# Pooled attention, routed experts and a dense layer in one kernel: scatters at spaced steps of their own, row squares on ScalarE, key differences and PV's evacuation one step up

## The chip, the cores and the metric

One core of a Trainium2 chip runs the whole program in one launch. The metric is the device time in microseconds (us) of one execution; lower is better. Engines are named as in the profile: PE (TensorE matmul), PEld (its weight loads), DVE (VectorE), ACT (ScalarE), POOL (GpSimd), SP (SyncE, which issues most DMAs).

## What is computed

The reference chains three blocks. Attention has 4 batches of 8 heads, 1152 rows of 64, and queries pooled by two (so 576 output rows a head). A router then sends each of the 2304 rows of 512 to one of 8 experts; last comes a dense layer with a squared ReLU.

```python
q_pool = q.reshape(B, H, S // 2, 2, D).mean(axis=3)
scores = scale * np.matmul(q_pool, k.transpose(0, 1, 3, 2))
attn = softmax(scores); x = attn @ v          # rows to (B*S/2, 512)
xn = x / (norm(x) + 1e-6); logits = xn @ en.T / tau
e = argmax(logits); y = gate[e] * (relu(x @ w1[e]) @ w2[e])
h = y @ w_in; out = (relu(h) ** 2) @ w_out
```

## The kernel before, in words

The order of the work is written out by hand. `Attention.run` lays every piece of work at a pair (step, rank), sorts the pairs and emits them. A pair of heads `h` (16 of them, called a head below) owns 18 steps that begin at step 18·h; parts of it lie earlier or later by the offsets of the table `PLAN`. Each engine takes its own instructions in the order in which they were emitted, and waits for the others by semaphores.

In one step of a head the PE makes a tile of scores (`scores`, two PSUM banks `st` in turn), ACT takes the exponential (`exps`, L412), and DVE or POOL makes the low half of the result (`low`, L422, `pl`). PV (L459) follows from step 13 in three groups of six steps; `evac` (L481 to L500) then divides a group by its row sums on DVE and writes it to `xb` (the rows of the batch): four instructions spread over two steps, of which `rs`, `rc` come first and the write `xb` a step later. Meanwhile the next head is prepared: `prep` splits keys, queries and values in a high and a low half (ACT L237, DVE L239), and `smax` finds each row's maximum: PE L338 multiplies queries with the keys and with `kd`, the difference of two halves of the keys (`kdiff`, DVE L315); ACT L361 (`rd`) and DVE L364 fold them to maxima.

When a batch is done (after heads 3, 7 and 11) a generator, `Route.steps`, takes its rows through the router, one piece at each step of the list `PLAN["route"]`, at rank 7, behind the step's other work: the row square sums `sq` (DVE, L661), `scale` (L898, L901), a high half on ACT (`hi`, L674) and a low half on DVE (`lo`) in the tile `xhl`, a transpose, the logits, `choose` (ten small pieces, the last writes the row indices `ri`) and then `scatter` (L761): an indirect DMA issued by POOL for each of 4 or 5 tiles, one a piece. `xhl` has a single buffer for all batches, so that `hi` of a batch waits for the scatters of the one before. In steps of the program these pieces lie so:

| batch | squares | scatters before | scatters in the change | `hi` of the next batch |
|---|---|---|---|---|
| 0 | 90 to 93 | 134, 135, 135, 135 | 135, 138, 141, 144 | 168 |
| 1 | 159 to 163 | 224 to 228 | 225, 227, 229, 231, 233 | 239 |
| 2 | 231 to 234 | 264, 265, 265, 266 | 266, 268, 270, 272 | behind the attention |

Behind batch 2's pieces follows `Moe.begin`: seven pieces that find the fullest expert, at steps 266 to 269 before. The SP reads its number and loads that expert's weights (`wraw`), which ACT splits (`wkr`, L1610) between the exponentials of the last head. The last batch goes through the router behind the attention (with squares of 384 columns). From about 500 us on come the experts and the dense layer, which no edit touches.

Of the kernel before, what the change touches and what calls it, by code (L numbers as in the profile page):

```python
# [10 lines left out]
BF16 = mybir.dt.bfloat16  # L11
I32 = mybir.dt.int32
U32 = mybir.dt.uint32
ACTF = mybir.ActivationFunctionType
ALU = mybir.AluOpType
# [88 lines left out]
        ],  # L104
    ],
    "due": [6, 10, 6],
    "init": [
        44, 45, 46, 47, 48, 49, 50, 51, 52, 53, 54, 55, 56, 57, 58, 59, 60, 61, 62, 63,
# [27 lines left out]
class Attention:  # L136
# [3 lines left out]
    def __init__(self, ctx, kctx, pctx, tc, q, k, v, xbp, xdone):  # L140
        self.tc, self.nc = tc, tc.nc
        self.q, self.k, self.v = q, k, v
        self.xdone = xdone
        B, H, S, D = q.shape
        assert S == 1152 and D == 64
        self.B, self.H = B, H
        self.HP = H // 2
        self.NP = B * self.HP
        pool = lambda n, b, **kw: ctx.enter_context(tc.tile_pool(name=n, bufs=b, **kw))
        keys = lambda n, b: kctx.enter_context(tc.tile_pool(name=n, bufs=b, side="right"))  # L150
        self.raw = keys("raw", 1)
        self.row = keys("row", 1)
        self.t1p = keys("t1", 3)
        self.r2p = pool("r2", 2)
        self.pp = pool("pp", 22)
        self.sm = pool("sm", 2)
        self.xbp = xbp
        self.per = pool("per", 1)
        psum = lambda n, b: pctx.enter_context(tc.tile_pool(name=n, bufs=b, space=PSUM))
        self.ps_t = psum("ps_t", 2)  # L160
        self.ps_m = psum("ps_m", 4)
        self.ps_v = psum("ps_v", 2)
        self.t2 = [self.per.tile([128, 18, 128], F16, name=f"t2_{i}") for i in range(2)]
        self.qr2 = [self.per.tile([128, 9, 128], F16, name=f"qr2_{i}") for i in range(2)]
        self.vx = [self.per.tile([128, 18, 130], F16, name=f"vx_{i}") for i in range(2)]
        self.st = {}

    def init(self):
        V = self.nc.gpsimd
# [137 lines left out]
    SMAX = [(n, m) for r in ((0, 1, 2, 3), (4, 5, 6, 7), (8,)) for n, m in  # L307
            [(r, 2)] + [(n, m) for n in r for m in (1, 0)]]

    def kdiff(self, h):  # L310

        s = self.st[h]
        kd = s["kd"] = self.sm.tile([128, 2, 512], BF16, tag="m24", name="kd")
        t1 = s["t1"].rearrange("p (a c) b -> p a (c b)", a=2)
        self.nc.vector.tensor_tensor(  # L315
            out=kd, in0=t1[:, :, 512:1024], in1=t1[:, :, 0:512], op=ALU.subtract
        )

    def smax(self, h, i):
# [195 lines left out]
    def steps(self, h):  # L515

        t = dict(PLAN["mid"], **PLAN.get(h, {}))
        t["pv"] = [[13 + 6 * g + m for m in range(6)] for g in range(3)]
        t["evac"] = [[13 + 6 * g + 6, 13 + 6 * g + 8] for g in range(3)]
        if h == self.NP - 2:  # L520
            t["evac"][2] = [31, 31]
        if h == self.NP - 1:
            t["pv"] = [[13 + m for m in range(9)]] * 3
            t["evac"] = None
        return 18 * h, t

    def run(self, extra):

        ev = {}

        def at(u, rank, f):
            ev.setdefault(u, []).append((rank, len(ev[u]) if u in ev else 0, f))

        def spread(u, rank, f):

            box = []

            def step():
                if not box:
                    box.append(f())  # L540
                next(box[0], None)

            for k in range(7):
                at(u + k // 3, (rank, 4.6, 6.5)[k % 3], step)

        for u, f in extra:
            at(u, 8, f)
        for h in range(self.NP):
            e0, t = self.steps(h)
            at(e0 + t["load"], 0, lambda h=h: self.load(h))  # L550
            at(e0 + t["load_v"], 0, lambda h=h: self.load_v(h))
            for n, d in enumerate(t["prep"]):
                at(e0 + d, 5, lambda h=h, n=n: self.prep(h, n))
            at(e0 + t["t2"], 0, lambda h=h: self.copy_t2(h))
            for i in range(21):
                u = e0 + (i if i < 18 else t["x"][i - 18])
                at(u - 1, 1, lambda h=h, i=i: self.scores(h, i))
                at(u, 2, lambda h=h, i=i: self.exps(h, i))
                at(u + 1, 6, lambda h=h, i=i, dve=i in t["low"]: self.low(h, i, dve))
            at(e0 + t["smax"][0], 4.4, lambda h=h: self.kdiff(h))  # L560
            for i, u in enumerate(t["smax"]):
                at(e0 + u, 4.5, lambda h=h, i=i: self.smax(h, i))
                spread(e0 + u + 1, 2.2, lambda h=h, i=i: self.smax_red(h, i))
            for g in range(3):
                k = len(t["pv"][g])
                for m, u in enumerate(t["pv"][g]):
                    a, b = (27 * m) // k, (27 * (m + 1)) // k
                    at(e0 + u, 4, lambda h=h, g=g, a=a, b=b: self.pv(h, g, a, b))
                if t["evac"]:
                    f = lambda h=h, g=g: self.evac(h, g)  # L570
                    if h == self.NP - 2 and g == 2:
                        at(e0 + t["evac"][g][1], 2.6, lambda f=f: list(f()))
                    else:
                        spread(e0 + t["evac"][g][1], 2.6, f)
            if h % self.HP == self.HP - 1 and h < self.NP - 1:
                box = []

                def step(b=h // self.HP, box=box):
                    if not box:
                        box.append(self.xdone(b))  # L580
                    next(box[0], None)

                for k in PLAN["route"][h // self.HP]:
                    at(e0 + 33 + k, 7, step)
        for u in sorted(ev):
            for _, _, f in sorted(ev[u], key=lambda t: t[:2]):
                f()
# [17 lines left out]
ORDER = ((0, 1, 2, 3), (0, 1, 2, 3, 4), (0, 1, 2, 3), (0, 4, 1, 2, 3))  # L605
# [39 lines left out]
class Route:  # L645
# [12 lines left out]
    def sq(self, i, cols=slice(0, 512), add=0.0):  # L658
        n = cols.stop - cols.start
        x = self.tiles[i][:, cols]  # L660
        self.nc.vector.tensor_tensor_reduce(  # L661
            out=self.t([512], "sq", BF16)[:, 0:n], in0=x, in1=x, scale=1.0, scalar=add,
            op0=ALU.mult, op1=ALU.add, accum_out=self.m.ss[:, self.s0 + i:self.s0 + i + 1],
        )

    def scale(self, a=0, b=None):
# [104 lines left out]
    def steps(self):  # L771

        n = self.n
# [23 lines left out]
                step += 4  # L797
                due[i] = step + PLAN["due"][BASE.index(self.s0)]
        yield from self.choose()
        for i in range(n):  # L800
            self.scatter(i)
            yield


class Moe:
# [906 lines left out]
def build(tc, q, k, v, emb, tau, w1, w2, w_in, w_out, consts, at, out):  # L1712
    nc = tc.nc
    pool = lambda c, n, b, **kw: c.enter_context(tc.tile_pool(name=n, bufs=b, **kw))
    with ExitStack() as ctx, tc.manual_schedule():
# [3 lines left out]
        with ExitStack() as actx:  # L1719
# [10 lines left out]
            def xdone(b):  # L1730
                xts = lambda i: rb.tile([128, 8, 128], F16, tag="xT", name="xT", bufs=2)
                xhl = rb.tile([128, 5, 1024], F16, tag="xhl", name="xhl")
                yield from route(b, slice(0, len(ORDER[b])), xts, xhl).steps()
                if b == 2:
                    yield from moe.begin(small)

# [146 lines left out]
```

## Time and profile before

| | us |
|---|---|
| median of three timed runs | 1180.41 |
| lowest and highest of them | 1174.77, 1183.54 |
| the profiled execution, its own time | 1168.99 |
| its span in the profile | 1167.0 |
| attention, first to last exponential | 25.1 to 464.7 |

The span is that of the profiled execution; 1.99 us lie outside it. In rows of a timeline the numbers are start and duration in us, and a bracket says how long the engine had been idle and who released it. In a row that groups instructions the numbers behind the bar are busy us and the mean duration in ns. Rows of a head's window run from its first exponential to that of the next head, 18 steps.

### The profile page before, as it was taken

To read this page: it belongs to the slowest core of one execution; us is meant where nothing else is said; L and a number is where in the kernel's file an instruction comes from. 1 tells how busy PE (TensorE), PEld (TensorE's weight loads), DVE (VectorE), ACT (ScalarE), POOL (GpSimd) and SP (SyncE) were. 2 spreads that over 40 slices of the span, in tenths; PEclk is the share of its full clock that TensorE was granted. 3 is DMA by queue.
4 is the path that set the end of the run, shared out by engine and by line. 5 is a ranking of instruction groups with operands and counts; after the bars stand their busy time and mean duration, and the time that the engine had idled before them with its cause. 6 is when DMAs were issued, how large, how long until landed. Compare 5 with 4: busy or idle time off the path is not lost. (4 is left out here: it accounts for less than half of the span.)

```text
span 1167.0 us, 28582 instructions
## 1 busy us (share of the span) xinstructions
PE 1046.6 (90%) x11297; PEld 702.0 (60%) x11340; DVE 734.8 (63%) x1403; ACT 521.7 (45%) x972; POOL 519.3 (45%) x454
## 2 busy tenths in 40 slices
PE   6889999988999798999998869787879999999996
PEld 2455665655666466999898858654435454555543
DVE  6898999999999988866654547958822121211200
ACT  4777777767777566323222325533303131221300
POOL 3655564555666456522442336826623232232300
PEclk7899998999999898999999889989889999999999
DMA  7555875755675435659558595323300000000000
GB/s 195 141 130 145 201 169 108 170 147 118 140 151 150 72 96 161 166 176 224 103 111 210 135 256 167 89 72 111 111 19 10 19 10 10 19 10 19 1 28 27
DMA packets 166245, 128.17 MB, mean 110 GB/s; under 512 B 125208, under 2 KB 129432, under 8 KB 166064
## 3 DMA queue, kind: packets, MB, share of 16 engines
q1 hardware_dynamic: 160304, 107.91, 39.0%
q0 software_dynamic: 5760, 17.85, 5.0%
q8 instruction: 113, 1.85, 0.7%
q14 instruction: 68, 0.56, 0.2%
HBM read 74.69 MB, written 12.60 MB: 75 GB/s over the span
## 5 line engine op out<-in xcount | busy, mean ns | idle before, releaser
L422 POOL TENSOR_TENSOR pl<-p 128x512 f16<-128x512 f32 x144 | 167.9, 1170 | 176.2 <-ACT p L412 173.3
L394 PE MATMUL st<-r,t 128*128 128x64 f16 (+3 forms) x1152 | 202.6, 299 | 5.4 <-ACT p L412 4.7
L412 ACT ACTIVATE p<-st 128x512 f32<-128x512 f32 x288 | 168.5, 595 | 78.9 <-PE st L394 77.1
L1465 PE MATMUL a<-yT,win 128*128 128x384 f16 x1056 | 178.5, 332 | 16.8 <-ACT r L1470 11.8
L459 PEld LDWEIGHTS <-p 128*128 128x128 bf16 x2304 | 135.6, 99 | 68.1 <-issue 18.5
L1465 PEld LDWEIGHTS <-win 128*128 128x128 f16 (+1 forms) x1152 | 114.8, 100 | 97.3 <-issue 27.1
L459 PE MATMUL pv<-vx,p 128*128 128x65 f16 x2250 | 160.0, 197 | 9.5 <-DVE xb L500 9.5
L1543 PE MATMUL o<-wo,gh 128*128 128x512 f16 (+1 forms) x513 | 154.5, 380 | 5.7 <-ACT wo L1168 4.2
L459 PE MATMUL pv<-vx,pl 128*128 128x65 f16 x1125 | 144.9, 194 | 0.0
L422 DVE TENSOR_TENSOR pl<-p 128x512 f16<-128x512 f32 x144 | 141.8, 985 | 1.0 <-ACT p L412 0.7
L1470 ACT ACTIVATE r<-a 128x384 f32<-128x384 f32 x88 | 42.9, 487 | 194.8 <-PE a L1465 128.7
L1483 POOL TENSOR_TENSOR gl<-r,gh 128x384 f16<-128x384 f32 x88 | 87.3, 997 | 79.8 <-ACT gh L1482 79.8
L1471 DVE TENSOR_TENSOR r<-r 128x384 f32<-128x384 f32 x88 | 59.5, 676 | 100.2 <-ACT r L1470 100.2
L364 DVE CUSTOM_DVE_ANT_0 rd<-sm,rd,mc 128x512 bf16<-128x512 f32 x144 | 106.7, 744 | 22.4 <-PE sm L338 9.1
L1405 PE MATMUL fsm<-x,ws 128*128 128x192 f16 (+1 forms) x1344 | 104.7, 241 | 17.6 <-issue 9.8
L1550 DVE TENSOR_SCALAR ot<-o,cms 128x512 f32<-128x512 f32 x18 | 13.5, 751 | 166.5 <-PE o L1543 166.5
L394 PEld LDWEIGHTS <-t 128*128 128x128 f16 (+1 forms) x1152 | 77.0, 100 | 66.5 <-issue 32.0
L1405 PEld LDWEIGHTS <-ws 128*128 128x128 f16 (+1 forms) x1344 | 100.6, 101 | 20.8 <-issue 12.2
L459 PEld LDWEIGHTS <-pl 128*128 128x128 f16 x1152 | 111.0, 101 | 0.0
L361 ACT ACTIVATE rd<-sm 128x512 bf16<-128x512 f32 x144 | 85.5, 597 | 52.7 <-PE sm L338 43.6
L1417 PEld LDWEIGHTS <-ws 128*128 128x128 f16 (+1 forms) x1344 | 97.5, 99 | 18.1 <-issue 14.5
L1417 PE MATMUL fst<-hl,ws 128*128 128x192 f16 (+1 forms) x448 | 96.9, 236 | 12.7 <-issue 8.8
(249 smaller groups left out, 1735.3 us busy)
## 6 DMA issues: line engine op xcount, KB each, us to landing
stg<-in_moe_w SPq DMA_DIRECT2D x24, 1024.0 KB, 7.7
vr<-in_v SPq DMA_DIRECT2D x16, 576.0 KB, 4.2
kr<-in_k SPq DMA_DIRECT2D x15, 576.0 KB, 5.3
fill<-in_moe_w_in POOLq DMA_DIRECT2D x16, 512.0 KB, 7.0
g<-in_moe_w_out SPq DMA_DIRECT2D x16, 512.0 KB, 3.5
qr<-in_q SPq DMA_DIRECT2D x15, 512.0 KB, 5.7
t<-t SPq DMA_DIRECT2D x16, 288.0 KB, 3.8
xs<-tmp SPq DMA_DIRECT2D x16, 192.0 KB, 2.8
```

The source lines that it names most:

```text
L361: nc.scalar.activation(out=s["rd"], in_=ps, func=ACTF.Relu)
L364: nc.vector.tensor_tensor_reduce(out=rd, in0=ps, in1=rd, scale=1.0, scalar=mc[:, slots:slots + 1], op0=ALU.add, op1=ALU.max, accum_out=mx[ ...
L394: nc.tensor.matmul(out=st[:, j * n:j * n + n], lhsT=lhs[0:kk, m, :], rhs=r[0:kk, c0:c0 + n], start=first, stop=(kk == 65), skip_group_chec ...
L412: nc.scalar.activation(out=p, in_=st[:, 0:p.shape[1]], func=ACTF.Exp, scale=SCALE)
L422: eng.tensor_tensor(out=pl, in0=s.pop(("p32", i)), in1=s["ph", i], op=ALU.subtract)
L459: nc.tensor.matmul(out=o[:, 0:vn], lhsT=s[p, i][:, cs:cs + w], rhs=vx[:, 9 * a_ + c, v0:v0 + vn], start=(u == 0 and p == "ph" and v0 == 0) ...
L1405: self.nc.tensor.matmul(out=ps[:, f, 0:w], lhsT=w1(wh, f2)[:, fs], rhs=x[:, 4 * xh + k, 0:w], start=(f == 0 and m == 0), stop=(m == 11), s ...
L1417: self.nc.tensor.matmul(out=yp[m // 2][:, m % 2, 0:w], lhsT=w2(wh, f)[:, ds], rhs=h(l, f), start=(f == i == m % 2 == 0), stop=(f == 7 and ...
L1465: nc.tensor.matmul(out=ps, lhsT=half(self.win[wh][:, k, fs], wh), rhs=self.yT[yh][:, k, c0], start=(m == 0), stop=(m == 11),)
L1471: nc.vector.tensor_tensor(out=r, in0=r, in1=r, op=ALU.mult)
L1483: self.nc.gpsimd.tensor_tensor(out=lo, in0=g, in1=hi, op=ALU.subtract)
L1543: nc.tensor.matmul(out=ps, lhsT=at(l, f)[:, rs], rhs=half(wout[wh][:, f], wh), start=(m == 0), stop=(m == 47),)
```

## The change

There are four edits. `scatter` leaves the generator: `run` emits it at steps of its own (`PLAN["scatter"]`, rank 7.5, with the object kept in `att.routes`); `Moe.begin`, which came behind the scatters, moves up by two steps (264 to 267). The 13 squares of 512 columns of batches 0 to 2 become one ACT instruction each with its accumulator; each took two on DVE, the product and the reading of the accumulator. `kdiff` is emitted one step earlier, and for head 0 in two halves. All of `evac` moves up by one step (its first instruction from eight to seven steps behind the group's first PV step), save that of head 14's last group.

```diff
+    "scatter": [[48, 51, 54, 57], [66, 68, 70, 72, 74], [35, 37, 39, 41]],
...
-    def kdiff(self, h):
+    def kdiff(self, h, a=slice(0, 2)):
...
-        kd = s["kd"] = self.sm.tile([128, 2, 512], BF16, tag="m24", name="kd")
+        if a.start == 0:
+            s["kd"] = self.sm.tile([128, 2, 512], BF16, tag="m24", name="kd")
...
-            out=kd, in0=t1[:, :, 512:1024], in1=t1[:, :, 0:512], op=ALU.subtract
+            out=s["kd"][:, a], in0=t1[:, a, 512:1024], in1=t1[:, a, 0:512], op=ALU.subtract
...
-        t["evac"] = [[13 + 6 * g + 6, 13 + 6 * g + 8] for g in range(3)]
+        t["evac"] = [13 + 6 * g + 7 for g in range(3)]
...
-            at(e0 + t["smax"][0], 4.4, lambda h=h: self.kdiff(h))
+            if h:
+                at(e0 + t["smax"][0] - 1, 4.4, lambda h=h: self.kdiff(h))
+            else:
+                for i, a in ((0, slice(0, 1)), (9, slice(1, 2))):
+                    at(e0 + t["smax"][i], 4.4, lambda a=a: self.kdiff(0, a))
...
+                for i, k in enumerate(PLAN["scatter"][h // self.HP]):
+                    at(e0 + 33 + k, 7.5, lambda b=h // self.HP, i=i: self.routes[b].scatter(i))
...
+        if n == 512:
+            self.nc.scalar.activation(out=out, in_=x, func=ACTF.Square, accum_out=ss)
+            return
...
-        for i in range(n):
-            self.scatter(i)
-            yield
```

PE and SP keep their instructions and their order. On POOL, around the scatters of batch 0 (`pl`, `plx` are low halves, `qs` the query sums of the next head), the order before was:

```order
L422 TENSOR_TENSOR pl<-p_4657 128x512
L761 DMA xs<-xhl,ri 18432x1024 x4
L422 TENSOR_TENSOR pl<-p_4724 128x512
L422 TENSOR_TENSOR pl<-p_4804 128x512
L422 TENSOR_TENSOR plx<-p32x 128x384
L259 TENSOR_TENSOR qs<-qr 128x576
L422 TENSOR_TENSOR pl<-p_4858 128x512
```

and it is now, at the same place:

```order
L425 TENSOR_TENSOR pl<-p_4660 128x512
L774 DMA xs<-xhl,ri 18432x1024
L425 TENSOR_TENSOR pl<-p_4726 128x512
L425 TENSOR_TENSOR pl<-p_4796 128x512
L425 TENSOR_TENSOR plx<-p32x 128x384
L774 DMA xs<-xhl,ri 18432x1024
L261 TENSOR_TENSOR qs<-qr 128x576
L425 TENSOR_TENSOR pl<-p_4853 128x512
L774 DMA xs<-xhl,ri 18432x1024
L425 TENSOR_TENSOR pl<-p_4934 128x512
```

Three of the four scatters went behind low halves that used to follow them. On DVE, where batch 1's squares began (`mc`, `rs`, `rc` small; `xb<-pv,rc` the write of PV's last group of the batch), the order before was:

```order
L373 TENSOR_SCALAR qr_0_105<-mx 128x4
L355 TENSOR_REDUCE mc<-sm 128x4
L481 TENSOR_SCALAR rs<-pv 128x3
L485 RECIPROCAL rc<-rs 128x3
L239 SCALAR_TENSOR_TENSOR krow<-kr,krow 128x9x64
L422 TENSOR_TENSOR pl<-p_5482 128x512
L661 ISA sq,ss<-xb 128x512
L661 ISA ss 128x1
L500 TENSOR_TENSOR xb<-pv,rc 128x3x64
L661 ISA sq,ss<-xb 128x512
L661 ISA ss 128x1
L364 ISA rd,mx<-sm,rd,mc 128x512
```

and it is now:

```order
L484 TENSOR_SCALAR rs<-pv 128x3
L488 RECIPROCAL rc<-rs 128x3
L376 TENSOR_SCALAR qr_0_105<-mx 128x4
L358 TENSOR_REDUCE mc<-sm 128x4
L503 TENSOR_TENSOR xb<-pv,rc 128x3x64
L241 SCALAR_TENSOR_TENSOR krow<-kr,krow 128x9x64
L425 TENSOR_TENSOR pl<-p_5483 128x512
L367 ISA rd,mx<-sm,rd,mc 128x512
```

The write to `xb` went ahead of a key split and a low half, and the squares are gone. They stand on ACT now, each ahead of an exponential:

```order
L364 ACTIVATE rd<-sm 128x512
L239 ACTIVATE krow<-kr 128x9x64
L673 ACTIVATE sq,ss<-xb 128x512
L415 ACTIVATE p_5586<-st 128x512
L673 ACTIVATE sq,ss<-xb 128x512
L415 ACTIVATE p_5612<-st 128x512
L364 ACTIVATE rd<-sm 128x512
```

The second square of a batch (in batches 1 and 2 the first too) waits for DVE's write to `xb`; the exponentials stand behind it.

## Rows read from the trace of the kernel before

**Rows 1.** The page's busy time by engine.
```profile
PE 1046.6 (90%) x11297; PEld 702.0 (60%) x11340; DVE 734.8 (63%) x1403; ACT 521.7 (45%) x972; POOL 519.3 (45%) x454
```

**Rows 2.** Windows by head: us, busy PE PEld DVE ACT POOL, clock, DMA, GB/s.
```profile
138.10:162.60 24.50, 23.93 (x378) 15.76 (x377) 22.71 (x51) 19.45 (x38) 15.71 (x13) 1.00 0.73 167
162.60:192.10 29.50, 26.55 (x377) 16.79 (x375) 27.10 (x59) 20.69 (x40) 14.90 (x13) 0.88 0.52 121
...
243.40:272.90 29.50, 25.53 (x377) 16.36 (x375) 27.39 (x59) 19.52 (x38) 16.74 (x15) 0.94 0.47 112
272.90:303.00 30.10, 25.64 (x374) 16.20 (x373) 28.87 (x65) 20.61 (x39) 16.46 (x13) 0.94 0.55 119
...
354.10:379.90 25.80, 23.92 (x384) 15.77 (x383) 24.47 (x57) 18.75 (x35) 15.69 (x15) 1.00 0.66 173
379.90:414.50 34.60, 26.83 (x383) 16.97 (x383) 32.66 (x68) 20.42 (x39) 16.93 (x16) 0.85 0.44 81
```

**Rows 3.** Waits of the PE, 0 to 430 us: total us, times, longest.
```profile
PE sm L338 <- DVE kd L315: 15.1, 13, 3.0
PE pv L459 <- DVE xb L500: 9.5, 7, 5.1
PE sm L338 <- DVE mx L364: 7.7, 6, 3.3
```

**Rows 4.** Timeline of the PE: five of those waits.
```profile
13.34 0.58 PE L338 MATMUL sm<-kd,r 128*128 128x512 bf16 x1 [3.01 <-DVE kd L315]
...
177.80 0.61 PE L338 MATMUL sm<-kd,r 128*128 128x512 bf16 x1 [2.27 <-DVE kd L315]
...
246.92 0.38 PE L338 MATMUL sm<-kd,r 128*128 128x512 bf16 x1 [3.27 <-DVE mx L364]
...
289.47 0.61 PE L338 MATMUL sm<-kd,r 128*128 128x512 bf16 x1 [1.99 <-DVE kd L315]
...
387.43 0.27 PE L459 MATMUL pv<-vx,p 128*128 128x65 f16 x2 [5.14 <-DVE xb L500]
```

**Rows 5.** Timeline of DVE: one low half as usual, four stretched instructions.
```profile
236.98 0.69 DVE L422 TENSOR_TENSOR pl<-p 128x512 f16<-128x512 f32 x1
...
238.60 7.59 DVE L422 TENSOR_TENSOR pl<-p 128x512 f16<-128x512 f32 x1
...
378.88 3.73 DVE L373 TENSOR_SCALAR qr<-mx 128x4 f16<-128x4 f32 x1
...
383.38 2.51 DVE L239 SCALAR_TENSOR_TENSOR krow<-kr,krow 128x576 f16<-128x576 f32 x1
...
441.67 4.97 DVE L422 TENSOR_TENSOR pl<-p 128x512 f16<-128x512 f32 x1 [0.15 <-ACT p L412]
```

**Rows 6.** Timeline of POOL around batch 0's scatters: first scatter, the train behind.
```profile
232.62 1.12 POOL L761 DMA_INDIRECT xs<-xhl,ri  x1 [2.02 <-DVE ri L756]
...
237.69 2.05 POOL L422 TENSOR_TENSOR pl<-p 128x512 f16<-128x512 f32 x2
...
244.61 1.03 POOL L422 TENSOR_TENSOR pl<-p 128x512 f16<-128x512 f32 x1
```

**Rows 7.** The squares on DVE (ns: shortest, median, longest); ACT instructions of their size.
```profile
L661 DVE CUSTOM_DVE_ANT_0 sq<-xb x16: 546/691/1525, 165.2 to 471.2; 128x512 bf16<-128x512 f32 x12, 128x384 bf16<-128x384 f32 x4
L1610 ACT ACTIVATE wt<-p 128x512 f16<-128x512 f32 x4 | 2.3, 616 | 0.0
```

**Rows 8.** Timeline of POOL: batch 1's last scatter.
```profile
377.77 1.27 POOL L761 DMA_INDIRECT xs<-xhl,ri  x1 [0.17 <-issue]
```

**Rows 9.** DMA issues by line: the scatters, with median us to landing.
```profile
xs<-xhl,ri POOLq DMA_INDIRECT x18, 3.6
```

**Rows 10.** Timeline of ACT from batch 2's squares to the first expert weights.
```profile
379.93 1.08 ACT L412 ACTIVATE p<-st 128x512 f32<-128x512 f32 x2
...
395.26 0.71 ACT L674 ACTIVATE xhl<-xb,sc 128x512 f16<-128x512 f32 x1
...
445.37 1.06 ACT L1610 ACTIVATE wkr<-wraw 128x1024 f16<-128x1024 f32 x1 [2.69 <-DMA wraw<-in_moe_w]
```

More of the change, by code (lines that the diff above doesn't have):

```diff
@@ L166, in __init__ @@
         self.st = {}
+        self.routes = {}
     def init(self):
@@ L518, in steps @@
         t["pv"] = [[13 + 6 * g + m for m in range(6)] for g in range(3)]
-        t["evac"] = [[13 + 6 * g + 6, 13 + 6 * g + 8] for g in range(3)]
+        t["evac"] = [13 + 6 * g + 7 for g in range(3)]
         if h == self.NP - 2:
-            t["evac"][2] = [31, 31]
+            t["evac"][2] = 31
         if h == self.NP - 1:
@@ L571, in run @@
                     if h == self.NP - 2 and g == 2:
-                        at(e0 + t["evac"][g][1], 2.6, lambda f=f: list(f()))
+                        at(e0 + t["evac"][g], 2.6, lambda f=f: list(f()))
                     else:
-                        spread(e0 + t["evac"][g][1], 2.6, f)
+                        spread(e0 + t["evac"][g], 2.6, f)
             if h % self.HP == self.HP - 1 and h < self.NP - 1:
@@ L660, in sq @@
         x = self.tiles[i][:, cols]
+        out = self.t([512], "sq", BF16)[:, 0:n]
+        ss = self.m.ss[:, self.s0 + i:self.s0 + i + 1]
+        if n == 512:
+            self.nc.scalar.activation(out=out, in_=x, func=ACTF.Square, accum_out=ss)
+            return
         self.nc.vector.tensor_tensor_reduce(
-            out=self.t([512], "sq", BF16)[:, 0:n], in0=x, in1=x, scale=1.0, scalar=add,
-            op0=ALU.mult, op1=ALU.add, accum_out=self.m.ss[:, self.s0 + i:self.s0 + i + 1],
+            out=out, in0=x, in1=x, scale=1.0, scalar=add, op0=ALU.mult, op1=ALU.add, accum_out=ss,
         )
@@ L1732, in xdone @@
                 xhl = rb.tile([128, 5, 1024], F16, tag="xhl", name="xhl")
-                yield from route(b, slice(0, len(ORDER[b])), xts, xhl).steps()
+                att.routes[b] = route(b, slice(0, len(ORDER[b])), xts, xhl)
+                yield from att.routes[b].steps()
                 if b == 2:
```

## The prediction, made before the change was run

> **What bounds the kernel now.** I read the busy times first. The PE is busy 90% of the span and DVE 63% [rows 1], which says little, since the edits touch the attention alone. So I cut that stretch into one window a head [rows 2]. Six heads are clean: 24.5, 26.4, 24.9, 25.1, 26.0 and 25.8 us (the first and the last are shown), 25.5 on the mean, with the PE at its full granted clock. Four are long: 29.5, 29.5, 30.1 and 34.6 us. In these DVE is busy for 27 to 33 us, three to eight more than in the clean heads shown, and the granted clock falls to 0.94, even to 0.85, which means that part of the head ran at 1.2 instead of 2.4 GHz. The long heads are those of the edits: 162.6 has batch 0's squares, 243.4 the work behind batch 0's scatters, 272.9 batch 1's squares, and 379.9 the work behind batch 1's scatters together with batch 2's squares.
>
> The PE's waits come next [rows 3]. The three largest groups all end with DVE: 15.1 us with the key differences `kd`, 9.5 with PV's evacuation, 7.7 with a maximum. Their times [rows 4] lie in the long heads: 2.27 us behind batch 0's squares, 1.99 behind batch 1's, 3.27 and 5.14 behind the scatters. DVE is late there for two reasons. It makes the squares itself, 13 of them, median 691 ns, up to 1525 [rows 7]. And some of its instructions are stretched: a low half that takes 0.69 us took 7.59, others 3.73, 2.51 and 4.97 [rows 5]. The first of these ended at 246.2 us, half a microsecond after POOL had ended a train of low halves that ran from 237.7 to 245.6 us without a gap, right behind the four scatters that began at 232.6 [rows 6]. The scatters had put POOL behind; it then caught up back to back, and DVE got no turn.
>
> **The change, part by part.** The sum goes against the profiled execution's own 1168.99 us.
>
> Squares. DVE loses 13 instructions (and 13 short reads of the accumulator) of 0.55 to 1.5 us, about 4 us in each of three heads. The head at 162.6 could fall by 4.0 us to a clean one, that at 272.9 by 4.6. ACT gains them. An ACT instruction of that size took 616 ns [rows 7]; whether the accumulator adds to it no row shows. I bound it by nothing and by a second pass, so 0.62 to 1.24 us, and take 0.62, the nearest row. Four cost 2.5 us in a head in which ACT is busy 20.7 of 29.5 us [rows 2], which has room; but they stand ahead of four exponentials in a row, on which the PE waits with two score banks, about one step (25.5/18 = 1.4 us) of slack. I charge half, 1.3 us a head. Gain: 4.0 - 1.3 = 2.7 and 4.6 - 1.3 = 3.3.
>
> Here a rule speaks against the edit. The Trainium skill (ScalarE: Activation LUTs, "Rules for kernel authors") says to put multiplications on VectorE, not ScalarE, which it holds to be up to about three times faster per element in bf16. By it the move loses: two thirds of 616 ns for each of 13 is 5.3 us, an estimate, and the sum below would be about 15 instead of 20. The rows have it the other way round: 616 ns on ACT against a median of 691 on DVE, for fp32 input.
>
> Scatters. POOL has the same work, now with a low half or two between any two scatters. In [rows 6] DVE's low halves ran in 0.69 us as long as POOL was among scatters [rows 5], and were stretched only behind them. So I expect shorter trains and most of the 6.9 us (7.59 - 0.69) back. Head 243.4: 3.0 of the 4.0 us above a clean head; bounds 0 and 4.0. Head 379.9: 34.6 - 25.5 = 9.1 us to gain, less 1.3 for ACT's squares and 2.0 for what is left of the stretching (a third of 3.73 + 2.51 [rows 5]): 5.8, bounds 0 and 9.1. A cost may come in: batch 1's last scatter moves from step 228 to 233. It now began at 377.8 and landed in 3.6 + 1.3 us [rows 8, 9], so near 382.7; ACT wrote `xhl` anew at 395.3 [rows 10]. Five steps take 7 us of those 12.6, and the time that the heads gain takes most of the rest. I charge nothing; at worst ACT waits some 2 us once.
>
> Key differences one step up. Of the 15.1 us [rows 3] 3.0 fall at the start [rows 4], 6.0 in the long heads (counted above: three waits, 2.27 and 1.99 the longest), and 6.1 in nine other waits. The wait goes with one step of lead, but DVE has no less to do; I take half, 3.0, bounds -1 (DVE in front of keys that have not landed) and 6.1. At the start the first half need not wait for the second half of the keys: 3.0 us at most. But the second half now stands behind a key split of head 1, whose keys must first land; I take 1.5, bounds 0 and 3.0.
>
> Evacuation one step up. It issues nothing new and passes no queue but DVE's own. PV's waits of 9.5 us lie mostly in the long heads, counted above; elsewhere I give it nothing. What hides it is that DVE is behind the PE at that place; were it not, `rs` would wait for PV and hold up the maxima behind it.
>
> `Moe.begin` two steps up. SP needs the expert's number for its first weights, and ACT waited 2.69 us for them ahead of `wkr`, with an exponential behind [rows 10]. Two steps of that stretch are about 2 us; I take 1.3, bounds 0 and 2.7.
>
> Sum: 2.7 + 3.3 + 3.0 + 5.8 + 3.0 + 1.5 + 1.3 = 20.6; less 0.6 for key differences that may wait for their keys in an early head, 20. So 1168.99 becomes 1149. The three timed runs before have a median of 1180.41, 11.4 above the profiled one; with the same 20 us off I forecast 1160. All upper bounds together are 4.0 + 4.6 + 4.0 + 9.1 + 6.1 + 3.0 + 2.7 = 33.5, or 1147; the forecast's own range is 1147 to 1168.
>
> **The rivals.** First: the scatters' spacing brings nothing. For it speaks that POOL's work is the same and fills the steps concerned nearly whole, so that its trains may only move; against it, that the stretched instructions all lie behind scatters [rows 5, 6]. Then heads 243.4 and 379.9 keep their length but for the squares (9.1 falls by 2.7, as in 162.6), and DVE, still the bound there, gives back the key differences elsewhere: 2.7 + 3.3 + 2.7 + 1.5 + 1.3 - 0.6 = 10.9, or 1169.5, on the border of no change. With half of the starting gain gone as well, 1171. The Trainium skill's page SBUF — State Buffer ("Who interferes with whom") leans to this side: the port pair that DVE and GpSimd share is locked for one whole instruction, so a blocked one loses at most one of POOL's, and the length of a train would not matter. The trace disagrees: 7.59 us is the time of a whole train.
>
> Second, on the other side: ACT becomes the bound. It works in order, and the squares wait for DVE's write to `xb`, with the exponentials behind. At batch 2 ACT was past 380 us [rows 10] when DVE's write let the PE go on at 387.4 [rows 4], 7 us of lag. If such a lag comes at two of the three batches, ACT stands still for 14 us and makes 13 squares for 8, and the heads with squares grow by these 22 us, the PE falling to its lower clock behind it as in 379.9. With what is left of the gains (3.0 + 1.5 + 1.3 - 0.6 = 5.2) the time is 1180.4 + 16.8 = 1197; with one such batch 1190. Against it: the write moves ahead of a square, a low half and a key split, over 2 us of DVE's work. The point from which it decides is DVE's lag at the second square: below two steps, 2.8 us, ACT hardly waits. That ScalarE is the wrong place for a square, as the rule above has it, would end here too.
>
> Third: the edits do what they say, but the PE's own waits only pass to its next releaser, such as the row transposes or the scores behind ACT. Then about half of the 20 comes, 1170, as in the first.
>
> **How the numbers follow.** A measurement of this kernel tells about 1% (12 us) from no change, as its three runs differ by 0.7%. I give the forecast 0.63, the first and the third rival together 0.28, the second 0.09. The forecast lies 1.7% below, and its range ends at the 1% bound (1168.6); the first and third end within 1%; the second ends about 1% above or beyond, and I leave 0.01 of it within. So faster 0.63, same 0.29, slower 0.08. The range runs from 1147 to 1177: it leaves out the second rival and little of the others.
>
> **What would show it.** Right: no window of a head above 28 us; no DVE instruction above 4 us in the attention; the PE's wait for `kd` under 5 us; ACT's squares near 0.6 us each, without idle time ahead of them above 1 us; `wkr` without its wait. Wrong: POOL trains of six or more instructions behind the spaced scatters with DVE stretched beside them; ACT idle ahead of a square until DVE's `xb`; ACT's first `xhl` of batch 2 waiting for a scatter; long heads at a clock below 0.95 as before.

## The result, and the profile after

The changed kernel took 1163.4 us (median of 4 runs, 1159.9 to 1171.1) against 1177.8 for the old one (4 runs): a ratio of 0.988, 95% interval 0.984 to 0.993. That is 14 us faster, just beyond the 1% from which a difference can be told here. A second set of runs of the same code (`c_after`, below) gave 0.987. The ratios leave out executions marked as slow, more than 1.5% above the fastest of the same kernel, so that they can differ by some us from the medians of all runs, which stand beside them where that matters. The forecast was 1160 with a range of 1147 to 1177, so time and sign came out as said. The parts did not, as the experiments show.

The changed kernel's profiled execution took 1162.62 us, span 1160.7. That is only 6.4 us below the old one's 1168.99, from which the sum of 20 us was taken: the old kernel's profiled execution lies 9 us below the median of its runs. The busy times, to set beside [rows 1]:

```profile
PE 1046.4 (90%) x11297; PEld 704.0 (61%) x11340; DVE 726.8 (63%) x1378; ACT 528.5 (46%) x998; POOL 530.8 (46%) x454
```

DVE lost 8 us and 25 instructions, ACT gained 7 us and 26. The windows by head answer to [rows 2]. In order: a clean head, batch 0's squares, the work behind batch 0's scatters, batch 1's squares, then the two heads with batch 1's scatters and batch 2's squares.

```profile
129.80:155.10 25.30, 23.84 (x375) 15.71 (x374) 25.10 (x54) 19.35 (x37) 16.14 (x13) 1.00 0.79 188
155.10:184.50 29.40, 28.10 (x375) 17.40 (x374) 24.65 (x54) 22.71 (x48) 15.64 (x14) 0.83 0.51 121
236.90:266.30 29.40, 27.18 (x378) 17.31 (x377) 28.53 (x55) 21.20 (x42) 19.11 (x17) 0.88 0.59 134
266.30:290.90 24.60, 23.49 (x366) 15.33 (x367) 22.79 (x52) 21.48 (x45) 15.17 (x13) 1.00 0.59 140
341.10:375.10 34.00, 29.65 (x403) 18.45 (x402) 28.75 (x64) 21.37 (x43) 20.09 (x19) 0.85 0.54 132
375.10:400.60 25.50, 24.42 (x374) 16.04 (x375) 23.72 (x55) 20.65 (x41) 13.84 (x13) 0.94 0.51 109
```

Only batch 1's squares brought their head down to a clean one (30.1 to 24.6). The head of batch 0's squares kept its 29.4 us although DVE is busy for 24.65 us in it now, and no longer for 27.1: there the PE itself is busy for 28.10 us, at a granted clock of 0.83. Now the waits of the PE from 0 to 430 us, to set beside [rows 3]:

```profile
PE st L397 <- ACT p L415: 8.8, 13, 2.6
PE sm L341 <- DVE mx L367: 8.3, 11, 2.2
PE sm L341 <- DVE kd L318: 7.4, 4, 3.9
PE pf L745 <- DVE oh L739: 5.1, 3, 3.1
```

The waits for `kd` fell from 15.1 to 7.4 us, of which 3.9 lie at the start (below), and those for `xb` from 9.5 to none. What took part of their place is the first row: waits of the scores for ACT's exponentials, 2.1 us in 4 before, 8.8 in 13 now. Three single waits, in the timeline of the PE:

```profile
17.22 0.61 PE L341 MATMUL sm<-kd,r 128*128 128x512 bf16 x1 [3.91 <-DVE kd L318]
...
162.77 0.54 PE L397 MATMUL st<-r,t 128*128 128x64 f16 x12 [0.99 <-ACT p L415]
...
374.65 0.80 PE L397 MATMUL st<-r,t 128*128 128x512 f16 x2 [2.65 <-ACT p L415]
```

The second and third lie behind ACT's squares of batch 0 and batch 2. ACT there (the last square of batch 0, the second of batch 2):

```profile
161.48 0.66 ACT L673 ACTIVATE sq<-xb 128x512 bf16<-128x512 f32 x1
162.00 0.23 ACT L673 ACTIVATION_READ_ACCUMULATOR sq<-xb 128x1 f32 x1
162.09 0.62 ACT L415 ACTIVATE p<-st 128x512 f32<-128x512 f32 x1
...
373.40 0.63 ACT L673 ACTIVATE sq<-xb 128x512 bf16<-128x512 f32 x1 [2.22 <-DVE xb L503]
```

A square has a read of the accumulator behind it, an instruction of its own, and takes 0.61 us of ACT's time in all (161.48 to 162.09). The 2.22 us are the second rival's wait for DVE's `xb`, once. Last, the stretched instructions of DVE, to set beside [rows 5]:

```profile
236.15 2.13 DVE L241 SCALAR_TENSOR_TENSOR krow<-kr,krow 128x576 f16<-128x576 f32 x1
...
238.21 2.31 DVE L425 TENSOR_TENSOR pl<-p 128x512 f16<-128x512 f32 x1
...
241.11 1.99 DVE L241 SCALAR_TENSOR_TENSOR krow<-kr,krow 128x576 f16<-128x576 f32 x1
...
366.75 3.63 DVE L425 TENSOR_TENSOR pl<-p 128x512 f16<-128x512 f32 x1
```

The single 7.59 us is gone. In its place stand three of about 2 us, each beside one of the spaced scatters, which began at 235.5 and 240.1 us, or beside POOL's work between them. The last row lies beside a scatter of batch 1. POOL's train is not gone, as the timeline of POOL shows with its first and last instruction:

```profile
231.89 1.01 POOL L774 DMA_INDIRECT xs<-xhl,ri  x1 [0.16 <-issue]
...
241.42 1.05 POOL L425 TENSOR_TENSOR pl<-p 128x512 f16<-128x512 f32 x1
```

Between the two stand seven more, two of them scatters, and no gap is above 0.17 us: 10.6 us of work nearly without a break, against 13.0 in the old kernel from the first scatter (232.62) to the end of the low halves.

### The profile page after: what moved, and what is told of

It reads as the page before. It is cut to its first block, busy times and chain, and to the rows that moved or that the text cites. A ratio compares the mean times of both kernels' runs of the same rounds, so it can differ in the third digit from the quotient of the medians.

```text
span 1160.7 us, 28581 instructions
## 1 busy us (share of the span) xinstructions
PE 1046.4 (90%) x11297; PEld 704.0 (61%) x11340; DVE 726.8 (63%) x1378; ACT 528.5 (46%) x998; POOL 530.8 (46%) x454
## 5 line engine op out<-in xcount | busy, mean ns | idle before, releaser
L425 POOL TENSOR_TENSOR pl<-p 128x512 f16<-128x512 f32 x144 | 175.6, 1224 | 155.3 <-ACT p L415 149.8
L1415 PE MATMUL fsm<-x,ws 128*128 128x192 f16 (+1 forms) x1344 | 108.9, 247 | 20.6 <-issue 14.5
L1415 PEld LDWEIGHTS <-ws 128*128 128x128 f16 (+1 forms) x1344 | 104.3, 104 | 24.5 <-issue 16.2
L1427 PEld LDWEIGHTS <-ws 128*128 128x128 f16 (+1 forms) x1344 | 97.5, 99 | 17.2 <-issue 15.7
L1427 PE MATMUL fst<-hh,ws 128*128 128x192 f16 (+1 forms) x896 | 100.7, 237 | 6.8 <-issue 5.6
```

The lines of the kernel that those rows point to most:

```text
L425: eng.tensor_tensor(out=pl, in0=s.pop(("p32", i)), in1=s["ph", i], op=ALU.subtract)
L1415: self.nc.tensor.matmul(out=ps[:, f, 0:w], lhsT=w1(wh, f2)[:, fs], rhs=x[:, 4 * xh + k, 0:w], start=(f == 0 and m == 0), stop=(m == 11), s ...
L1427: self.nc.tensor.matmul(out=yp[m // 2][:, m % 2, 0:w], lhsT=w2(wh, f)[:, ds], rhs=h(l, f), start=(f == i == m % 2 == 0), stop=(f == 7 and ...
```

## The experiments

Theory 1 is the prediction's sum. Theory 2 was read from how far the changed kernel's trace runs ahead of the old one's. All ratios are to the old kernel, whose median stayed at 1176 to 1178 us, so 0.001 is 1.2 us.

One table holds what the traces say by stage. Its times run from the start of ACT's third 384-column exponential (`p32x`) in the head before to the same instruction in the head itself, the heads counted from 0; for the changed kernel's head 5, for instance, from head 4's to its own:

```profile
152.10 0.49 ACT L415 ACTIVATE p32x<-st 128x384 f32<-128x384 f32 x1
...
181.53 0.49 ACT L415 ACTIVATE p32x<-st 128x384 f32<-128x384 f32 x1
```

which is 29.4. The first column runs from the span's start to this instruction of head 1. "Other heads" are 2, 3, 4, 6, 10 and 11. Each row is one execution, so a column tells something where several rows agree.

```
           start  other  5: sq   7+8:    9: sq  12+13: scat  14+15: scat b2,
                  heads  b0      scat b0 b1     b1, sq b2    expert start
old         78.9  157.8  29.5    54.6    30.2   60.8         50.0
changed     71.9  157.5  29.4    53.5    25.8   59.2         48.3
c_after     77.9  158.6  29.5    55.1    25.8   59.0         47.1
u_sq        72.2  157.2  27.8    57.7    29.8   62.5         48.4
u_scat      72.9  157.5  29.6    54.0    25.8   59.5         57.7
u_kd        78.8  163.3  25.9    53.4    26.5   60.2         47.2
u_evac      73.3  159.3  29.4    55.0    27.1   60.4         46.5
kd0         76.7  158.1  29.5    55.2    25.8   61.2         48.3
sq_sp       77.9  158.9  26.5    55.8    25.7   54.5         48.1
dbl_scat    71.8  157.2  25.3    54.3    25.8   62.3         49.1
b_scat      78.5  157.5  29.5    61.2    30.2   59.5         48.9
b_sq        78.1  159.2  25.9    53.5    27.9   62.5         55.4
b_kd        77.1  157.3  26.5    56.8    29.8   57.9         56.5
best        78.8  158.8  26.5    53.2    25.7   57.9         56.9
```

### `c_after`: the changed kernel again

> The changed kernel once more, unedited, for more executions and a second profile. All theories: 1159 to 1168 and 0.985 to 0.992 of the old kernel. If the lead over the old kernel along the attention is a property of the code, its first nine heads repeat to within 1.5 us (5.3 in the first head, 7.0 in the second, 7.5 in the fifth, 7.8 in the ninth); what differs after that is scatter from execution to execution and no part of the change.

Ratio 0.987 (0.982 to 0.991). The lead did not repeat: the start took 77.9 us in place of 71.9, with not an instruction changed. In this execution the PE waited longer in several places, among them 4.73 us in place of 3.91 for the first head's second half of `kd`, and 1.95 us at 46.3 us for row transposes of head 1, for which it hardly waited in the first (0.17 us at 42.1). So 6 us of the 12 by which the first trace of the changed kernel led at the last evacuation (465.5 against 477.5 us) come and go with the execution. From head 2 on the two agree to some 2 us in every column. Behind the attention, from the expert table's matmuls to the first of the experts' second layer, code that no edit touches took 177.5 us in the old kernel, 183.2 in the changed, and between 174.0 and 184.7 in the others: as much scatter again. One pair of traces can't settle a few us here; stage by stage over many, it can.

### `u_sq` and `b_sq`: the squares undone, and alone

```diff
-        if n == 512:
-            self.nc.scalar.activation(out=out, in_=x, func=ACTF.Square, accum_out=ss)
-            return
```

> The changed kernel with all square sums back on VectorE. The changed kernel's median is 1163.4 us. Theory 1 (the sum of the prediction): the squares on ScalarE are worth 2.7 + 3.3 = 6.0 us, so 1169.4. Theory 2 (read from how far the changed kernel runs ahead of the old one along the attention: 7.5 us before and 7.5 us behind the squares of batch 0, 6.6 and then 12.1 us at those of batch 1, 11.4 and then 15.2 at those of batch 2): nothing in batch 0, 5.5 in batch 1 and up to 3.8 in batch 2, so 1169 to 1173, and the head with the squares of batch 0 stays at about 29 us. Theory 3 (the burst on ScalarE costs as much as it relieves VectorE): 1163 to 1165.

Ratio 0.990 (0.987 to 0.994): 3 to 5 us lost of the 14 to 16 (1 to 3 by the medians of all runs), less than theories 1 and 2 had and more than theory 3. The interval, 1162 to 1170 us, leaves all three standing. `b_sq` puts the same lines into the old kernel:

> The old kernel with the square sums on ScalarE alone, at their old steps. Theory 1 (the prediction): 6.0, so 1171, 0.995. Theory 2 (undoing them cost 0.9904 against 0.987 to 0.988): 2 to 4 us, so 1173 to 1175, 0.997 to 0.998. If the parts only work together: 1177.

Ratio 0.995 (0.992 to 0.998): 5.9 us, as theory 1 said, with an interval from 2 to 10. The table shows where: head 9 takes 29.8 to 30.2 us in all four traces with the squares on DVE and 25.7 to 27.9 in all ten others.

### `sq_sp`: the squares at every second step

Of each line of the table only the start is shown.

```diff
-            3, 4, 5, 6, 7, 7, 8, 9, 10, 11, 12, 15,
+            1, 3, 5, 7, 8, 8, 9, 9, 10, 11, 12, 15,
...
-            0, 1, 2, 3, 4, 5, 6, 7, 8, 9, 10, 11,
+            0, 2, 4, 6, 7, 8, 8, 9, 9, 10, 10, 11,
...
-            0, 1, 2, 3, 4, 5, 6, 7, 8, 9, 10, 11,
+            1, 3, 4, 6, 7, 7, 8, 8, 9, 9, 10, 11,
```

> The changed kernel with the squares on ScalarE at every second step instead of every step. Theory A (four or five squares of about 0.85 us in as many steps make ScalarE late for TensorE's scores: waits of 0.99 at 162.77 and 2.65 at 374.65): those two waits go or fall below 0.5, the granted clock of the head with the squares of batch 0 is back above 0.9 and the head at 26 us; 3 to 5 us, so 1159. Theory B (the squares take ScalarE's slack, whatever their distance): the same as the changed kernel, 1161 to 1166.

Ratio 0.981 (0.977 to 0.985), 1156.7 us: the fastest kernel of the study, 6 to 8 us better than the changed one, and theory A's time holds: five of its six runs lie below all ten of the changed kernel (1157.4 us and more). Its mechanism is shown in part, as follows. Here is head 5, first the window and the waits in `c_after`:

```profile
159.20:188.70 29.50, 28.20 (x373) 17.52 (x373) 24.90 (x55) 22.76 (x48) 15.86 (x14) 0.83 0.52 121
```

```profile
PE st L397 <- ACT p L415: 1.2, 2, 1.0
```

then in `dbl_scat`, where this head has the code of `c_after`:

```profile
152.80:178.10 25.30, 23.61 (x364) 15.27 (x364) 24.14 (x51) 22.52 (x47) 16.29 (x14) 1.00 0.54 126
```

```profile
PE st L397 <- ACT p L415: 1.2, 2, 1.0
PE sm L341 <- DVE mx L367: 0.4, 1, 0.4
```

and in `sq_sp`:

```profile
158.70:185.20 26.50, 23.90 (x364) 15.37 (x363) 26.23 (x52) 22.40 (x47) 15.97 (x14) 1.00 0.55 128
```

```profile
PE sm L341 <- DVE mx L367: 1.8, 1, 1.8
PE st L397 <- ACT p L415: 0.4, 2, 0.2
```

All eight traces with the squares in a row on ACT have this same wait of 1.2 us. In five of them the granted clock fell behind it and the head took 29.4 to 29.6 us; in three (`u_kd`, `dbl_scat`, `b_sq`) it stayed at 1.00 and the head took 25.3 to 25.9. With the squares spaced (`sq_sp`, `best`) the wait is 0.4 us, the clock stayed at 1.00 both times, and the head took 26.5, with a wait of 1.6 to 1.8 us for a maximum at its end. Two of two against three of eight may be chance, so it is not shown that the spacing keeps the clock up; and the other part of `sq_sp`'s gain, in heads 12 and 13 (54.5 us against 59.0 to 59.2), is not in `best` (57.9). In the changed kernel the fall looks like this, in windows of the head before the wait's end, behind it, and after:

```profile
155.10:162.80 7.70, 6.49 (x92) 3.80 (x90) 7.63 (x15) 7.70 (x20) 3.91 (x4) 1.00 0.73 134
162.80:174.00 11.20, 11.20 (x116) 6.47 (x116) 6.95 (x17) 5.61 (x11) 2.87 (x3) 0.54 0.54 148
174.00:184.50 10.50, 10.42 (x172) 7.13 (x170) 10.06 (x24) 9.40 (x19) 8.86 (x7) 1.00 0.33 83
```

For 11.2 us the PE had no gap and ran almost all the time at 1.2 GHz. Against the three traces without the fall that cost some 4 us, behind a wait of 1.2.

### `u_scat`, `b_scat` and `dbl_scat`: the scatters undone, alone, and doubled

```diff
-                for i, k in enumerate(PLAN["scatter"][h // self.HP]):
-                    at(e0 + 33 + k, 7.5, lambda b=h // self.HP, i=i: self.routes[b].scatter(i))
...
         yield from self.choose()
+        for i in range(n):
+            self.scatter(i)
+            yield
```

> The changed kernel with the scatters back in the routing's own sequence, at the old steps (all of a batch within 2 to 5 steps; the start of the expert part goes back by two steps with them). Theory 1 (the prediction): the spacing is worth 3.0 + 5.8 and the earlier start of the expert part 1.3, so 1163.4 + 10.1 = 1173.5. Theory 2 (read from the lead of the changed kernel: 6.5 to 7.8 us across the scatters of batch 0, 12.6 to 8.7 across those of batch 1, 14.6 to 10.2 across those of batch 2): the spaced scatters give nothing over all, each of them lengthens a VectorE instruction by 1 to 3 us wherever it stands, so 1159 to 1165, and a train of VectorE instructions of over 4 us is back in the heads of the scatters.

Ratio 0.984 (0.979 to 0.988): no slower without the spacing. Stretched DVE instructions of over 4 us are back in batch 1 (4.37) and batch 2 (4.73), but in batch 0, where all four scatters stand together again, none is above 1.9. `b_scat` is the reverse edit on the old kernel:

> The old kernel with the spaced scatters alone (and the start of the expert part two steps earlier, which follows from them). The old kernel's median is 1177 us. Theory 1 (the prediction): 3.0 + 5.8 + 1.3 = 10.1, so 1167, a ratio of 0.991. Theory 2 (undoing them in the changed kernel made it 0.9837 against 0.987 to 0.988, no slower; a second set of 13 scatters cost some 5 us): the stretch of VectorE goes with each scatter, wherever it stands, so the spacing gives nothing: 1174 to 1179, 0.997 to 1.002. Theory 3 (the parts need each other: VectorE's trains were what held the old kernel, and only the squares' going made the spacing needless): 0.991 to 0.995 here.

Ratio 0.997 (0.993 to 1.000): 3.9 us, and not surely any. `dbl_scat` adds a scatter behind each:

```diff
                     at(e0 + 33 + k, 7.5, lambda b=h // self.HP, i=i: self.routes[b].scatter(i))
+                    at(e0 + 34 + k, 7.5, lambda b=h // self.HP, i=i: self.routes[b].extra(i))
```

> The changed kernel with each of the 13 scatters in the attention done a second time one step later, into a buffer of its own that nothing reads. Theory 1 (the prediction: GpSimd's work for a scatter stretches VectorE's instructions, 2 to 4 us each where they come together, and VectorE sets the heads' length): a second set costs at least what the spacing was to save, 9 us or more, so 1172 or above. Theory 2 (the stretch falls into VectorE's slack and TensorE's lead, which is why the spacing gave nothing): 0 to 4 us, so 1163 to 1167.

Ratio 0.993 (0.990 to 0.996): some 6 us slower than the changed kernel for 13 scatters, 0.5 us each, between the two theories. By the medians of all runs (1167.3 against 1163.4 and 1166.1) it is 1 to 4, so the price of a scatter is uncertain. Its trace is of the fastest of its twelve runs.

The table has two findings in one. For batch 0 the spacing gave nothing: heads 7 and 8 take 53.2 to 56.8 us with the old steps and 53.4 to 61.2 with the new (the 61.2, in `b_scat`, at a granted clock of 0.83 against 0.97 in the old kernel). But heads 14 and 15 take 46.5 to 49.1 in all nine traces with the new steps, and 55.4 to 57.7 in four of the five with the old ones, the old kernel's 50.0 being the exception. The cause is in DVE's work on the expert's number, here in the timeline of DVE in `u_scat`:

```profile
429.55 0.14 DVE L962 TENSOR_SCALAR taba<-mxa 128x1 int32<-128x1 f32 x1
430.02 4.73 DVE L425 TENSOR_TENSOR pl<-p 128x512 f16<-128x512 f32 x1 [0.33 <-ACT p L415]
434.68 1.00 DVE L967 TENSOR_SCALAR rank<-cst,mxa 128x8 f32<-128x8 f32 x1
435.60 0.14 DVE L971 TENSOR_SCALAR taba<-mxa 128x1 int32<-128x1 f32 x1
```

with ACT behind it,

```profile
440.06 1.06 ACT L1621 ACTIVATE wkr<-wraw 128x1024 f16<-128x1024 f32 x1 [5.62 <-DMA wraw<-in_moe_w]
```

and in the changed kernel:

```profile
424.69 0.14 DVE L961 TENSOR_SCALAR taba<-mxa 128x1 int32<-128x1 f32 x1
424.75 0.35 DVE L503 TENSOR_TENSOR xb<-pv,rc 128x192 f32<-128x192 f32 x1
425.14 0.69 DVE L425 TENSOR_TENSOR pl<-p 128x512 f16<-128x512 f32 x1
425.75 0.23 DVE L966 TENSOR_SCALAR rank<-cst,mxa 128x8 f32<-128x8 f32 x1
425.89 0.15 DVE L970 TENSOR_SCALAR taba<-mxa 128x1 int32<-128x1 f32 x1
```

```profile
432.36 1.05 ACT L1620 ACTIVATE wkr<-wraw 128x1024 f16<-128x1024 f32 x1
```

With the scatters close together, a DVE instruction beside POOL's train is stretched in the middle of this chain. From one `taba` write to the next it takes 6.1 us in `u_scat`, 5.8 in `best`, 9.0 in `b_kd` and 6.3 in `b_sq`; SP asks for the weights that much later, and ACT waits 5.6, 5.9, 6.5 and 6.0 us for them, with the PE's scores behind (5.5 us in `u_scat`). With the spaced ones the chain takes 1.2 us in the changed kernel (3.2 in `b_scat`, the longest, where ACT still waits 2.19 us). In the old kernel's trace the stretched instruction (the 4.97 of [rows 5], at 441.67) came a microsecond after the chain's end, and the wait was only 2.69.

Two edits go together here: in every run with the spaced scatters `Moe.begin` also starts two steps earlier, and in the changed kernel the first `taba` write (424.69) falls together with batch 2's first scatter (424.7), where in `u_scat` (429.55) it falls together with the last (429.4). No run parts the spacing from the earlier start, so which of them shortens the chain is not shown.

That `u_scat` is nevertheless no slower by its runs stays open: its profiled execution was the slowest of its six, and whether the others had the long wait no trace shows.

### `u_kd`, `kd0` and `b_kd`: the key differences

In `u_kd` all are back at the old step, in `kd0` that of the first head alone:

```diff
-            if h:
-                at(e0 + t["smax"][0] - 1, 4.4, lambda h=h: self.kdiff(h))
-            else:
-                for i, a in ((0, slice(0, 1)), (9, slice(1, 2))):
-                    at(e0 + t["smax"][i], 4.4, lambda a=a: self.kdiff(0, a))
+            at(e0 + t["smax"][0], 4.4, lambda h=h: self.kdiff(h))
```

> The changed kernel with the key differences at the old step of every head, whole in the first one too. Theory 1 (the prediction): 3.0 for one step and 1.5 for the first head, less 0.6, so 1163.4 + 3.9 = 1167.3. Theory 2 (the lead of the changed kernel is 5.3 us in the first head, 7.0 in the second and 7.4 in the third, before any square or scatter): 7 us, so 1170, with the waits of TensorE for the key differences back at 13 and some 15 us.

Ratio 0.994 (0.990 to 0.998): some 8 us lost (3 to 6 by the medians of all runs), and the waits are back, from 0 to 430 us:

```profile
PE sm L341 <- DVE kd L318: 13.1, 13, 3.0
```

> The changed kernel with the key difference of the first head whole at its old step; those of the other heads stay one step earlier. Theory 1 (the prediction): the two halves are worth 1.5 us, so 1165. Theory 2 (all of the first head's lead of 5.3 us comes from the halves, since with both key-difference edits undone it was 0.0): 5 us of the 7 that the undoing of both cost, so 1168, with a lead of 0 to 1 us in the first head and 1 to 2 in the third. Theory 3 (the step earlier also lifts the first head, by head 1's): the lead is 3 or more in the first head.

Ratio 0.983 (0.978 to 0.987): by its time the halves of the first head bring nothing that can be seen. Its 3.0 us wait had only gone over to the second half, 3.91 us behind head 1's key split. Theory 2's time falls here. Its lead does not: in the table's first column the five starts of 71.8 to 73.3 us all belong to traces with the halves (the other two of these have 77.9), and the seven without them have 76.7 to 78.9. So the halves seem to shorten the start by 5 us or so in most executions; why the runs of `kd0` show no loss stays open. `b_kd` moves the other heads' key differences in the old kernel:

> The old kernel with the key differences of all heads but the first one step earlier, alone. Theory 1 (the prediction): 3.0 less 0.6, so 1174.6, 0.998. Theory 2 (undoing both key-difference edits cost 0.994 against 0.987 to 0.988, undoing the first head's alone nothing): about 7 us, so 1170, 0.994, and TensorE's waits for key differences are 8 us or less instead of 15.

Ratio 0.989 (0.984 to 0.995): 12 us, with an interval of 7 to either side. TensorE's waits for key differences fall as theory 2 said, and by this edit alone, from 15.1 us to:

```profile
PE sm L338 <- DVE kd L315: 6.5, 5, 3.1
```

By its middle value the one step is the largest part of the change, but its interval overlaps with that of the squares (2 to 10 us), and no column of the table shows all of it. The plainest is "other heads": 163.3 in `u_kd` against 157.2 to 159.3 everywhere else; but the old kernel, `b_scat` and `b_sq` have the old step too and are not slow there, so this column settles nothing. What is slow in `u_kd` is head 3, 35.7 us long, with this row on DVE:

```profile
96.05 5.93 DVE L376 TENSOR_SCALAR qr<-mx 128x5 f16<-128x5 f32 x1
```

and POOL busy beside it with low halves, query sums and a memset, from

```profile
95.89 1.04 POOL L425 TENSOR_TENSOR pl<-p 128x512 f16<-128x512 f32 x1 [1.96 <-ACT p L415]
...
100.91 1.03 POOL L425 TENSOR_TENSOR pl<-p 128x512 f16<-128x512 f32 x1
```

The PE waited 5.5 us for maxima behind it. The first scatter came at 234.9 us, so the stretching needs no scatter: a train of other POOL work is enough.

### `u_evac`: the evacuation

```diff
-        t["evac"] = [13 + 6 * g + 7 for g in range(3)]
+        t["evac"] = [13 + 6 * g + 8 for g in range(3)]
```

> The changed kernel with PV's evacuation back at the old steps (one step later). Both theories that differ on the other parts give about nothing: 1163 to 1165 (the prediction costed it at 0). The rival: TensorE's waits for the evacuation, 9.5 us in 7 of the old kernel and 2.3 us in 1 of the changed one, go by this edit, so they come back here and the time is 1168 to 1172.

Ratio 0.985 (0.980 to 0.989): no slower, although the waits for `xb` are back, from 0 to 430 us:

```profile
PE st L397 <- ACT p L415: 12.8, 13, 5.2
PE sm L341 <- DVE kd L318: 5.7, 2, 5.0
PE pv L462 <- DVE xb L503: 4.1, 4, 2.3
PE sm L341 <- DVE mx L367: 3.0, 3, 2.2
...
PE pv L462 <- DVE xb L493: 2.7, 1, 2.7
```

The edit moves the PE's wait from one releaser to another; the maxima's waits fall from 8.3 to 3.0 as `xb`'s rise by 6.8. The exponentials' waits rise from 8.8 to 12.8, for the squares stand on ACT and wait for the later `xb`:

```profile
381.56 0.63 ACT L673 ACTIVATE sq<-xb 128x512 bf16<-128x512 f32 x1 [4.77 <-DVE xb L503]
```

In `b_sq`, with the old steps too, it is 4.68 us; in the eight other traces with squares on ACT the longest such wait is 0 to 3.2. So the earlier evacuation shortens the wait that the squares bring to ACT, though the runs show no time for it.

### `best`: squares spaced, first head whole, scatters back

> The changed kernel with the squares at every second step, the key difference of the first head whole, and the scatters back in the routing's own sequence. If what the single edits gave adds up (7 us from the squares' steps, 3 to 5 from each of the other two, which are both within their intervals): 1147 to 1152, a ratio of 0.975 to 0.979. If only the squares' steps are real: 1155 to 1158, 0.981 to 0.983. If the spaced scatters matter once ScalarE's burst is gone: 1159 or above.

Ratio 0.990 (0.987 to 0.994): worse than `sq_sp` by 10 us (7 by the medians). The last column has most of it: 56.9 us against 48.1, ACT waiting 5.9 us ahead of `wkr`, though this was the fastest of its eight runs. So the scatters' edit, with the earlier start of the expert part that goes with it, matters here for batch 2. That it matters only once ScalarE's burst is gone is not shown: `u_scat` and `b_sq` have the burst and the same wait. The first head's halves, the other difference, did not matter in `kd0`'s runs.

## Why the prediction was right, and where it was not

The total is right within 4 us, but by errors that offset one another: scatters priced at 8.8 us gave little that can be seen, key differences priced at 3.9 gave two to three times that, and only 14 of the 20 us came. That is in part luck. Alone on the old kernel, three parts gave 5.9 + 3.9 + 12.5 = 22 us; together they give 14 to 16. That they remove the same waits of the PE would explain it, but the three intervals (4, 4 and 7 us to either side) are too wide to show that they don't add up.

**The starting point. In part wrong.** The prediction called four heads long, all of them heads of the edits, among those from 138.1 us on. The two before, 28.7 us (81.0 to 109.7) and 28.4 (109.7 to 138.1), are long as well and hold neither squares nor scatters.

**Squares, batch 1: 3.3 us. Right.** Head 9 lost 4.4. The price of 0.62 us a square was right too: 0.61 on ACT's queue. On DVE the 13 squares took 0.68 to 1.53 us, six of them above 1.2 (the 546 ns of [rows 7] is of 384 columns). By the rule cited from the Trainium skill (ScalarE: Activation LUTs, "Rules for kernel authors") the prediction estimated a loss of 5.3; alone the move gained 5.9, so the rule, whose factor of three is for bf16 with one source, does not carry over to this fp32 square.

**Squares, batch 0: 2.7 us. Wrong.** ACT was charged 1.3 us a head for the exponentials behind the squares, and the PE waited 1.2. What the step left out is the granted clock behind that wait: 0.54 for 11.2 us. In five traces of eight it ate the gain; in the other three the head took 25.3 to 25.9 us, the gain that was forecast and a little more.

**Scatters: 3.0 + 5.8 us. Wrong: this is the step that failed.** It held that scatters a step or more apart would leave POOL no train, and with it DVE no stretched instruction. But POOL's work is the same and fills these steps: spaced, it still ran from 231.9 to 242.5 us without a gap above 0.17, three DVE instructions beside it took 2.0 to 2.3 us and one in batch 1 took 3.6, and the PE goes on waiting, for a maximum (1.82 us at 241.2, in place of 3.27). Batch 0 gained 1.1 us in the first trace and nothing over all of them; heads 12 and 13 gained 1.6, where spacing the squares as well (`sq_sp`) gained 6.3. Here the first rival ("the spacing brings nothing") had it right for two batches of three, and its reason too, that POOL's trains only move. The Trainium skill's SBUF — State Buffer ("Who interferes with whom") leaned that way, but the bound of one POOL instruction that the prediction drew from it does not hold: in `u_scat` a DVE instruction lost 4 us beside a train of instructions of 0.8 to 1.1 us, and in `u_kd` over 5.

**`Moe.begin`: 1.3 us. Wait right, size off.** The row it rested on, 2.69 us, was the kind end of a wait that was 5.6 to 6.5 us in four other traces with the old steps, and the stretched instruction that sets it stands beside POOL's train. Between heads 14 and 15 there and in the changed kernel lie 7 to 9 us; how they divide between the earlier start and the spacing no run shows.

**Key differences: 3.0 + 1.5 - 0.6 us. Undersized.** The runs give 8 and 12 us for the step, with wide intervals. The waits outside the start fell from 12.1 to 3.5 us; the prediction priced half of the 6.1 us outside the long heads, and most of these went, with part of the 6.0 inside them. The 1.5 for the first head's halves is nothing by the runs of `kd0` and about 5 us by the starts of the traces, and stays open.

**Evacuation: 0. Right**, for another reason than the one given: waits for `xb` did go, but others came.

**The rivals.** The second (ACT becomes the bound) came in one place, 2.22 us at batch 2's second square, below its own point of 2.8; in `kd0`, `b_sq` and `u_evac` the same wait was 3.2 to 4.8, above that point, and these kernels were still faster than the old one. The third (waits pass on) came in part: the waits for ACT's exponentials went from 2.1 to 8.8 us.

**The signs.** Right: no DVE instruction above 4 us, squares near 0.6 us, `wkr` without its wait, and no `xhl` of batch 2 waiting for a scatter. Wrong: four heads above 28 us, long heads below a clock of 0.95, 7.4 us of waits for `kd`, a square behind 2.22 us of idle time, and a POOL train of more than six instructions with DVE stretched beside it.

## What to carry to other kernels

When work moves to an engine that has room on the average, look at the steps where it lands: four squares in a row made the PE wait 1.2 us, and with them at every second step the kernel was another 6 to 8 us faster. Price a wait of the PE with the clock behind it, not alone. And where a term rests on one wait in one trace, ask what decides its length: here a stretched instruction came a microsecond too late to show a wait twice as long. Spreading work over the steps ends a train only where the engine has gaps to spread it into; POOL had none.

## What the runs showed of the hardware that was not expected

The same PE wait of 1.2 us, in the same code, was followed by a granted clock of about 0.5 in five profiled executions and by full speed in three; the heads took 29.4 to 29.6 and 25.3 to 25.9 us. What decides between the two no run shows. A DVE instruction of a few columns (128x5) took 5.93 us beside a POOL train with no scatter in it. The square's sum costs ACT an instruction of its own, `ACTIVATION_READ_ACCUMULATOR`, 186 to 250 ns long in the changed kernel, but it overlaps the square: the pair takes 0.61 us of the queue. And executions of the same code differ by 6 us up to the table's instruction of head 1, and by up to 10.7 us behind the attention.
